# First block of a fused convolution and feed-forward kernel: one third of the taps moved from VectorE to TensorE

## The chip, the cores and the metric

One core of a Trainium2 chip. The metric is the device time of one execution in microseconds; a kernel's time is the median of its runs. The profile's span is the time from the first to the last instruction, in most runs 1.6 to 1.9 us less than the device time. The granted clock is the share of TensorE's full clock that the profile records (0.50 is half clock).

## The reference

A depthwise causal convolution with seven taps over the sequence (the taps are a softmax of a small weight, one set per head), then a feed-forward layer with SiLU. 32768 tokens, 192 channels, 2048 hidden units. x and weight are float32; w_in and w_out come as float64, and the kernel turns their 64-bit words into float32 itself ("rounding" below).

```python
w = softmax(weight)                          # 8 heads x 7 taps
x_pad = concat([zeros(B, 6, D), x], axis=1)  # causal, B=8, S=4096, D=192
out[b, s, c] = sum_k w[head(c), k] * x_pad[b, s + k, c]
h = out.reshape(B * S, D) @ w_in             # 192 x 2048
return (h * sigmoid(h)) @ w_out              # 2048 x 192
```

## The kernel before

The tokens are worked off in 32 blocks of 1024. A block's channels are split in three thirds (k = 0, 1, 2) of 64; two halves of the block's tokens lie in partitions 0 to 63 and 64 to 127. For blocks 1 to 31 everything runs beside the products of the block before. For block 0 nothing can: it has to be loaded, transposed, convolved and copied out while the weights are loaded and rounded. The change touches that head only. Its parts:

```python
def turn_in(b, k):      # VectorE: transpose third k of block b, nats -> xts
def conv(b, k, i):      # tap i; tap 0 on ScalarE (blocks 0, 1), the rest on VectorE
    src = xts[b][:, k, i : i + TB]
    dst = nats[b][:, k, :, :]                # in place of the loaded data
    ... scalar_tensor_tensor(out=dst, in0=src, scalar=tap, in1=dst, mult, add)
def spread(b, k):       # 4 DMAs of 128 KB: the convolved third to both row halves (dup)
    for n in range(2):
        for e in range(2):
            nc.sync.dma_start(out=dups[b][R*e : R*e+R, n, k, :], in_=src[R*n : R*n+R, :])
def load_in(j, queue):  # 4 DMAs of 192 KB: raw words of quarter j of w_in
def round_in(j, k):     # VectorE, a little ScalarE: raw words -> wr[j]; after the last piece
    ...                 # of a quarter, 2 GpSimd DMAs ws[j] <- wr[j] (halves swapped)
def up_plain(0, 0):     # block 0, quarter 0: third by third into 8 PSUM banks
    for k, (a, n) in order:                  # k outermost for quarter 0
        for e in range(2):
            nc.tensor.matmul(hs[a, n, e], rows(wr[j], e)[:, a, k, :], rows(d, e)[:, n, k, :], ...)
... # (cut)
for k in range(NK):
    if k == 0:
        turn_in(0, 0)
        conv(0, 0, 0)
    for i in range(1, K):
        conv(0, k, i)
    spread(0, k)
    if k < NK - 1:
        for j in ((1, 2), (3,))[k]:
            load_in(j, nc.sync)
        turn_in(0, k + 1)
        conv(0, k + 1, 0)
    round_in(0, k)
round_in(1)
for j in range(NJ):
    up_plain(0, j)
    ...
```

In the trace the nc.sync queue issues in this order: dup of the first third, weights of quarters 1 and 2, dup of the second third, weights of quarter 3, a small copy (tail, 4.5 KB), dup of the last third. In the text, "dup" is the set of four copies of one convolved third, a copy "lands" when its completion is reported, and each float32 product makes two records in the profile.

Of the kernel before, what the change touches and what calls it, by code (L numbers as in the profile page):

```python
# [9 lines left out]
F32 = mybir.dt.float32  # L10
I32 = mybir.dt.int32
AF = mybir.ActivationFunctionType
ALU = mybir.AluOpType
# [4 lines left out]
def kernel(  # L18
# [24 lines left out]
    nc = tc.nc  # L43
# [3 lines left out]
    H, K = weight.shape  # L47
    NT = B * S
    DFF = moe_w_in.shape[1]
    P = 128  # L50
    R = 64
    NK = D // R
    grp = D // H
    pad = K - 1
    TB = 512
# [16 lines left out]
    gpool = ctx.enter_context(tc.tile_pool(name="gp", bufs=2 * NJ))  # L72
    upool = ctx.enter_context(tc.tile_pool(name="up", bufs=13))
# [29 lines left out]
    def pin(ins):  # L103
        return tc.keep_in_program_order(ins)
# [8 lines left out]
    vec, act = Pinned(nc.vector), Pinned(nc.scalar)  # L113

    def bank():
        return psum.tile([P, TB], F32, tag="ps", name="ps")

    nats, xts, gs = {}, {}, {}

    def load(b, ks=range(NK)):  # L120
# [14 lines left out]
        out=wexp.rearrange("p h k -> p (h k)"),  # L135
        in_=weight.rearrange("(o h) k -> o (h k)", o=1).to_broadcast([P, H * K]),
# [5 lines left out]
    for k in range(NK):  # L142
        nc.gpsimd.dma_start(
            out=xts[0][R:P, k, 0:pad], in_=x0[:, k, :], allow_slow_non_contiguous=True
# [11 lines left out]
    wr = [const.tile([P, 2, NK, P], F32, name=f"wr{j}") for j in range(NJ)]  # L156
# [5 lines left out]
    def raw_tile(key):  # L162

        pool, tag = (gpool, "g") if key in (("i", 2), ("i", 3)) else (tpool, "t")
        raws[key] = pool.tile([P, 4 * TB], I32, tag=tag, name="raw")[:, 0 : 2 * WC]
        return raws[key]

    def load_in(j, queue):
        raw = raw_tile(("i", j)).rearrange("p (a k c) -> p a k c", a=2, k=NK)
        for e in range(2):  # L170
            for a in range(2):
                c = 2 * P * (NM * a + 2 * j + e)
                queue.dma_start(
                    out=raw[R * e : R * e + R, a, :, :], in_=in32[:, :, c : c + 2 * P]
                )
# [53 lines left out]
    def round_in(j, k=None):  # L229

        words = raws["i", j].rearrange("p (a k c t) -> p a k c t", a=2, k=NK, t=2)
        if k is None:
            rounded(
                wr[j].rearrange("p a k c -> p a (k c)"),
                words.rearrange("p a k c t -> p a (k c) t"),
                j < 2,
            )
        else:
            rounded(wr[j][:, :, k, :], words[:, :, k], j < 2)
        if k in (None, NK - 1):  # L240

            del raws["i", j]
            for e in range(2):
                nc.gpsimd.dma_start(
                    out=ws[j][R * e : R * e + R], in_=wr[j][R - R * e : 2 * R - R * e]
                )
# [41 lines left out]
    for e in range(2):  # L288
        half = hot[R * e : R * e + R]
        for sign, base in ((1, 0), (-1, grp - 1)):  # L290
            nc.gpsimd.affine_select(
                out=half,
                in_=half,
                compare_op=ALU.is_ge,
                fill=0.0,
                base=base,
                pattern=[[sign * R, NK], [-sign * grp, H]],
                channel_multiplier=sign,
            )
    wred = const.tile([P, H], F32, name="wred")  # L300
    taps = const.tile([P, NK, K], F32, name="taps")
    each = const.tile([P, NK, K, H], F32, name="each")
# [22 lines left out]
    def turn_in(b, k):  # L325
        if k == 0 and b:
            xt = xts[b] = xpool.tile([P, NK, pad + TB], F32, tag="xt", name="xt")
            if b * TT % S == 0:
                nc.gpsimd.memset(xt[0:R, :, 0:pad], 0.0)
            else:  # L330
                nc.gpsimd.tensor_copy(xt[0:R, :, 0:pad], tails.pop(b))
        xt = xts[b]
        pin(
            nc.vector.transpose(  # L334
                xt[:, k, pad : pad + TB], nats[b][:, k, :, :].rearrange("p k c -> p (k c)")
            )
        )
        if k == NK - 1:
            if b:
                nc.sync.dma_start(out=xt[R:P, :, 0:pad], in_=xt[0:R, :, TB : TB + pad])  # L340
            if (b + 1) * TT % S:
                tails[b + 1] = xpool.tile([R, NK, pad], F32, tag="tail", name="tail", bufs=2)
                nc.sync.dma_start(out=tails[b + 1], in_=xt[R:P, :, TB : TB + pad])

    def conv(b, k, i):

        src = xts[b][:, k, i : i + TB]
        dst = nats[b][:, k, :, :].rearrange("p k c -> p (k c)")
        tap = taps[:, k, i : i + 1]
        if i == 0 and b < 2:  # L350
            pin(nc.scalar.activation(dst, src, AF.Copy, scale=tap))  # L351
        elif i == 0:
            pin(nc.vector.tensor_scalar(dst, src, scalar1=tap, scalar2=None, op0=ALU.mult))
        else:
            pin(
                nc.vector.scalar_tensor_tensor(  # L356
                    out=dst, in0=src, scalar=tap, in1=dst, op0=ALU.mult, op1=ALU.add
                )
            )

    def spread(b, k):

        if k == 0:
            dups[b] = xpool.tile([P, 2, NK, TB], F32, tag="dup", name="dup")
        src = nats[b][:, k, :, :].rearrange("p k c -> p (k c)")
        for n in range(2):
            for e in range(2):
                nc.sync.dma_start(
                    out=dups[b][R * e : R * e + R, n, k, :], in_=src[R * n : R * n + R, :]
                )  # L370
# [17 lines left out]
    def rows(t, e):  # L388
        return t[R * e : R * e + R]

    def g_tile(b, j, a):
        if (b, j, a) not in gs:
            gs[b, j, a] = gpool.tile([P, 2, 2, TB], F32, tag="g", name="g")
        return gs[b, j, a]

    def up_plain(b, j):

        d = dups[b]
        outs = [(a, n) for a in range(2) for n in range(2)]
        hs = {(a, n, e): bank() for a, n in outs for e in range(2)}  # L400
        order = [(k, o) for k in range(NK) for o in outs]
        if j:
            order = [(k, o) for o in outs for k in range(NK)]
        for k, (a, n) in order:
            for e in range(2):
                nc.tensor.matmul(  # L406
                    hs[a, n, e],
                    rows(wr[j], e)[:, a, k, :],
                    rows(d, e)[:, n, k, :],
                    start=k == 0,  # L410
                    stop=k == NK - 1,
                )
            if k == NK - 1:
                for e in range(2):
                    g = g_tile(b, j, a)
                    act.activation(g[:, n, e, :], hs[a, n, e], AF.Silu)
# [308 lines left out]
            store(0, cols)  # L725


    for k in range(NK):
        if k == 0:
            turn_in(0, 0)  # L730
            conv(0, 0, 0)
        for i in range(1, K):
            conv(0, k, i)
        spread(0, k)
        if k < NK - 1:
            for j in ((1, 2), (3,))[k]:
                load_in(j, nc.sync)
            turn_in(0, k + 1)
            conv(0, k + 1, 0)
        round_in(0, k)  # L740
    round_in(1)
    for j in range(NJ):
        up_plain(0, j)
        if j + 2 < NJ:
            round_in(j + 2)
            load_out(j, nc.sync)
        else:
            round_out(j + 2 - NJ)
            load_out(j, nc.sync)
        if j == 1:  # L750
            load(1)
# [63 lines left out]
```

## Time and profile before

| | before |
|---|---|
| median, 3 runs | 2420.47 us (2420.43 to 2420.83) |
| TensorE busy | 99% of the span, without a pause from 37.73 us to the last blocks |
| head, 0 to 37.73 us | three batches of products, at 16.66, 27.34 and 33.47 us |

How to read it: nothing after 37.73 us can change through an edit to block 0's convolution, so the effect of the change is the shift of that one moment. A sharp mark for it in every profile is the start of the first down projection (68.83 us before): from there to the end of the span all kernels below take 2349.4 to 2350.2 us. The lines are in the prediction.

### The profile page before, as it was taken

To read this page: it belongs to the slowest core of one execution; us is meant where nothing else is said; L and a number is where in the kernel's file an instruction comes from. 1 tells how busy PE (TensorE), PEld (TensorE's weight loads), DVE (VectorE), ACT (ScalarE), POOL (GpSimd) and SP (SyncE) were. 2 spreads that over 40 slices of the span, in tenths; PEclk is the share of its full clock that TensorE was granted. 3 is DMA by queue.
4 is the path that set the end of the run, shared out by engine and by line. 5 is a ranking of instruction groups with operands and counts; after the bars stand their busy time and mean duration, and the time that the engine had idled before them with its cause. 6 is when DMAs were issued, how large, how long until landed. Compare 5 with 4: busy or idle time off the path is not lost.

```text
span 2418.9 us, 43131 instructions
## 1 busy us (share of the span) xinstructions
PE 2388.1 (99%) x17776; PEld 936.7 (39%) x17776; DVE 2073.5 (86%) x2821; ACT 990.7 (41%) x1857; POOL 69.8 (3%) x98
## 2 busy tenths in 40 slices
PE   6999999999999999999999999999999999999998
PEld 3334433334433344333443333443334433334433
DVE  8889888898888888888988889888889888898876
ACT  3234533345433345333454334543334533345432
POOL 3300000000000000000000000000000000000000
PEclk9999999999999999999999999999999999999999
DMA  8321222222222212222222222122222222222220
GB/s 157 75 45 38 39 44 53 44 43 38 36 53 51 42 32 43 46 53 40 40 40 40 53 47 45 33 36 53 53 41 40 36 45 53 43 41 40 36 40 14
DMA packets 454085, 111.65 MB, mean 46 GB/s; under 512 B 423936, under 2 KB 429056, under 8 KB 453888
## 3 DMA queue, kind: packets, MB, share of 16 engines
q1 hardware_dynamic: 450064, 106.89, 23.8%
q8 instruction: 139, 2.28, 0.4%
q0 software_dynamic: 480, 1.58, 0.3%
q10 hardware_dynamic: 3344, 0.42, 0.1%
q14 instruction: 58, 0.48, 0.1%
HBM read 31.49 MB, written 25.17 MB: 23 GB/s over the span
## 4 chain that ended last, share of the span: by engine, by line
PE 98%; DVE 1%; ACT 0%; DMA 0%; SPq 0%; issue 0%; POOLq 0%; POOL 0%; ACTq 0%; DVEq 0%
PE ps L442 49%; PE ps L513 46%; PE ps L541 2%; PE ps L406 1%; DVE nat L356 0%; DMA nat<-in_x_dram 0%; SPq L127 0%; DVE two L111 0%; ACT two L111 0%; ACT g L111 0%; DVE cmb L111 0%; DVE osb L111 0%; DVE xt L334 0%; ACT nat L351 0%; ACT L111 0%
## 5 line engine op out<-in xcount | busy, mean ns | idle before, releaser
L442 PE MATMUL ps<-dup,ws 64*128 64x512 f32 x2480 | 869.9, 589 | 0.0
L513 PE MATMUL ps<-g,wo 128*32 128x512 f32 x2984 | 662.2, 592 | 0.0
L466 DVE TENSOR_TENSOR g<-u,ps 128x512 f32<-128x512 f32 x744 | 485.5, 679 | 119.2 <-PE ps L442 89.9
L442 PE MATMUL ps<-win,wr 64*128 64x512 f32 x1488 | 567.7, 589 | 0.0
L513 PE MATMUL ps<-t,wo 128*32 128x512 f32 (+1 forms) x4464 | 500.7, 450 | 0.0
L463 ACT ACTIVATE g<-g 128x512 f32<-128x512 f32 x744 | 444.6, 631 | 97.2 <-DVE g L466 97.2
L442 PEld LDWEIGHTS ps<-dup,ws 64*128 64x128 f32 x2480 | 363.0, 187 | 292.0 <-issue 277.9
L513 PE MATMUL ps<-t,wx 128*32 128x512 f32 x2976 | 452.9, 592 | 0.0
L356 DVE SCALAR_TENSOR_TENSOR nat<-xt,taps,nat 128x512 f32<-128x512 f32 x576 | 432.0, 750 | 18.7 <-ACT nat L351 3.8
L442 PE MATMUL ps<-dup,wr 64*128 64x512 f32 x992 | 419.9, 596 | 0.0
L457 ACT COPY u<-ps 128x512 f32<-128x512 f32 x496 | 278.1, 589 | 228.7 <-PE ps L442 225.8
L580 ACT COPY cmb<-ps 96x512 f32<-96x512 f32 x30 | 17.5, 582 | 805.5 <-PE ps L513 805.5
L483 DVE TENSOR_TENSOR t<-g,t 128x1024 f32<-128x1024 f32 x248 | 303.4, 1223 | 18.7 <-PE ps L513 8.3
L483 DVE TENSOR_TENSOR t<-g 128x1024 f32<-128x1024 f32 x248 | 299.6, 1219 | 23.0 <-PE ps L513 23.0
L442 PEld LDWEIGHTS ps<-win,wr 64*128 64x128 f32 x1488 | 233.4, 187 | 175.5 <-issue 147.2
L513 PEld LDWEIGHTS ps<-t,wo 128*32 128x32 f32 x4464 | 178.3, 110 | 222.6 <-issue 204.6
L442 PE MATMUL ps<-win,ws 64*128 64x512 f32 x496 | 242.2, 589 | 0.0
L513 PE MATMUL ps<-g,wx 128*32 128x512 f32 (+1 forms) x1512 | 234.6, 585 | 0.0
L513 PEld LDWEIGHTS ps<-t,wx 128*32 128x32 f32 x2976 | 121.9, 110 | 277.6 <-issue 268.4
L592 DVE TENSOR_TENSOR cmb<-cmb,ps 96x512 f32<-96x512 f32 x150 | 102.3, 682 | 135.3 <-ACT u L577 133.2
L442 PEld LDWEIGHTS ps<-dup,wr 64*128 64x128 f32 x992 | 160.5, 187 | 128.2 <-issue 114.3
L513 PEld LDWEIGHTS ps<-g,wo 128*32 128x32 f32 x2984 | 169.4, 110 | 98.3 <-issue 98.3
(66 smaller groups left out, 1206.4 us busy)
## 6 DMA issues: line engine op xcount, KB each, us to landing
dup<-nat SPq DMA_DIRECT2D x384, 128.0 KB, 2.3
nat<-in_x_dram SPq DMA_DIRECT2D x382, 64.0 KB, 2.4
out_dram<-osb SPq DMA_DIRECT2D x376, 64.0 KB, 2.0
raw<-in_moe_w_in_dram SPq DMA_DIRECT2D x16, 192.0 KB, 5.7
raw<-in_moe_w_out_dram SPq DMA_DIRECT2D x8, 384.0 KB, 3.7
ws<-wr POOLq DMA_DIRECT2D x8, 192.0 KB, 3.3
xt<-xt SPq DMA_DIRECT2D x31, 4.5 KB, 1.9
tail<-xt SPq DMA_DIRECT2D x24, 4.5 KB, 1.9
```

The lines of the kernel that those rows point to most:

```text
L356: nc.vector.scalar_tensor_tensor(out=dst, in0=src, scalar=tap, in1=dst, op0=ALU.mult, op1=ALU.add)
L406: nc.tensor.matmul(hs[a, n, e], rows(wr[j], e)[:, a, k, :], rows(d, e)[:, n, k, :], start=k == 0, stop=k == NK - 1,)
L442: nc.tensor.matmul(bk[b, m, bn], rows(w, half), rows(v, half), start=first, stop=True, skip_group_check=True,)
L457: pin(copy(u, bk[b, m, "1"]))
L463: pin(nc.scalar.activation(g, g, AF.Silu))
L466: pin(nc.vector.tensor_tensor(g, us.pop((b, m, i)), bk[b, m, bn], op=ALU.add))
L483: pin(nc.vector.tensor_tensor(t[i // 2][:, i % 2, :], u, v, op=ALU.subtract))
L513: nc.tensor.matmul(accs[b][i][SQ * q : SQ * q + SQ, to], lhs[:, e, SQ * k : SQ * k + SQ], rhs[:, e, ts(q, TB // 4) if i == 5 else to], sta ...
L541: nc.tensor.matmul(acc[k][R * n : R * n + R, :], wo[j][:, a, e, R * k : R * k + R], gs[b, j, a][:, n, e, :], start=j == 0 and a == 0 and e ...
L580: pin(nc.scalar.copy(c[0], acc[0][0:n, :]))
L592: pin(nc.vector.tensor_tensor(out_, u, v, op=ALU.add))
```

## The change

Intent: VectorE is busy all through the head. Six of its taps (the second third) become seven products on TensorE with diagonal matrices (taps on the diagonal), summed in PSUM; ScalarE makes the diagonals and copies the sum back. TensorE stood idle there. The second third is transposed after four taps of the first, so that TensorE can start early.

```diff
+    one_hot = upool.tile([P, TB], F32, tag="u", name="one_hot")[:, 0:P]
+    nc.gpsimd.memset(one_hot, 1.0)
+    for sign in (1, -1):
+        nc.gpsimd.affine_select(out=one_hot, in_=one_hot, ...)   # cut: leaves the diagonal
 ... (the products of up_plain are held in program order: pin(...))
-    for k in range(NK):
-        if k == 0:
-            turn_in(0, 0)
-            conv(0, 0, 0)
-        for i in range(1, K):
-            conv(0, k, i)
-        spread(0, k)
-        if k < NK - 1:
-            for j in ((1, 2), (3,))[k]:
-                load_in(j, nc.sync)
-            turn_in(0, k + 1)
-            conv(0, k + 1, 0)
-        round_in(0, k)
+    turn_in(0, 0)
+    conv(0, 0, 0)
+    diag = gpool.tile([P, K, P], F32, tag="g", name="diag")
+    for i in range(K):
+        act.activation(diag[:, i, :], one_hot, AF.Copy, scale=taps[:, 1, i : i + 1])
+    for i in range(1, 5):
+        conv(0, 0, i)
+    turn_in(0, 1)
+    for i in range(5, K):
+        conv(0, 0, i)
+    spread(0, 0)
+    for j in (1, 2):
+        load_in(j, nc.sync)
+    by_pe = bank()
+    for i in range(K):
+        pin(nc.tensor.matmul(by_pe, diag[:, i, :], xts[0][:, 1, i : i + TB],
+                             start=i == 0, stop=i == K - 1))
+    round_in(0, 0)
+    turn_in(0, 2)
+    conv(0, 2, 0)
+    round_in(0, 1)
+    act.copy(nats[0][:, 1, :, :].rearrange("p k c -> p (k c)"), by_pe)
+    spread(0, 1)
+    load_in(3, nc.sync)
+    for i in range(1, K):
+        conv(0, 2, i)
+    spread(0, 2)
+    round_in(0, 2)
     round_in(1)
```

More of the change, by code (lines that the diff above doesn't have):

```diff
@@ L299 @@
             )
+    one_hot = upool.tile([P, TB], F32, tag="u", name="one_hot")[:, 0:P]
+    nc.gpsimd.memset(one_hot, 1.0)
+    for sign in (1, -1):
+        nc.gpsimd.affine_select(
+            out=one_hot,
+            in_=one_hot,
+            compare_op=ALU.is_ge,
+            fill=0.0,
+            base=0,
+            pattern=[[-sign, P]],
+            channel_multiplier=sign,
+        )
     wred = const.tile([P, H], F32, name="wred")
@@ L405, in up_plain @@
             for e in range(2):
-                nc.tensor.matmul(
-                    hs[a, n, e],
-                    rows(wr[j], e)[:, a, k, :],
-                    rows(d, e)[:, n, k, :],
-                    start=k == 0,
-                    stop=k == NK - 1,
+                pin(
+                    nc.tensor.matmul(
+                        hs[a, n, e],
+                        rows(wr[j], e)[:, a, k, :],
+                        rows(d, e)[:, n, k, :],
+                        start=k == 0,
+                        stop=k == NK - 1,
+                    )
                 )
@@ L725, in finish @@
             store(0, cols)
-    for k in range(NK):
-        if k == 0:
-            turn_in(0, 0)
-            conv(0, 0, 0)
-        for i in range(1, K):
-            conv(0, k, i)
-        spread(0, k)
-        if k < NK - 1:
-            for j in ((1, 2), (3,))[k]:
-                load_in(j, nc.sync)
-            turn_in(0, k + 1)
-            conv(0, k + 1, 0)
-        round_in(0, k)
+    turn_in(0, 0)
[13 more added lines that the diff above has]
+    for i in range(K):
+        pin(
+            nc.tensor.matmul(
+                by_pe, diag[:, i, :], xts[0][:, 1, i : i + TB], start=i == 0, stop=i == K - 1
+            )
+        )
+    round_in(0, 0)
[9 more added lines that the diff above has]
+    round_in(0, 2)
     round_in(1)
```

## The prediction

> **What bounds the kernel now.** I read the page first, for the bound and the chain that ended last. Columns: engine, busy us, share of the span, instructions; then shares of the span.
>
> ```profile
> span 2418.9 us, 43131 instructions
> PE 2388.1 (99%) x17776; PEld 936.7 (39%) x17776; DVE 2073.5 (86%) x2821; ACT 990.7 (41%) x1857; POOL 69.8 (3%) x98
> PE 98%; DVE 1%; ACT 0%; DMA 0%; SPq 0%; issue 0%; POOLq 0%; POOL 0%; ACTq 0%; DVEq 0%
> ```
>
> TensorE is the bound, so only its idle time can be won. Where is that? The busy time by stretch (us of the stretch, busy us of each engine with instructions, granted clock, DMA share, GB/s):
>
> ```profile
> 0.00:16.60 16.60, 0.00 (x0) 0.00 (x0) 10.35 (x28) 3.79 (x7) 3.41 (x13) 1.00 0.78 124
> 16.60:37.70 21.10, 15.80 (x48) 7.33 (x48) 20.14 (x39) 6.99 (x13) 3.50 (x5) 0.92 0.91 186
> 37.70:110.00 72.30, 72.27 (x336) 29.63 (x336) 66.84 (x82) 21.49 (x37) 37.11 (x50) 1.00 0.40 93
> 110.00:2400.00 2290.00, 2290.00 (x17262) 895.58 (x17264) 1967.74 (x2660) 953.89 (x1792) 24.32 (x29) 1.00 0.23 43
> ```
>
> From 37.7 us on TensorE does not stop until the last blocks. The change touches the first block alone, so its whole effect is how far the moment moves at which TensorE starts its unbroken run (37.73 us, when the products of the first quarter of the up projection are done). The timeline of the first 40 us, TensorE, VectorE (DVE) and the queues (start, length, what; idle before and what ended it):
>
> ```profile
> 16.66 5.90 PE L406 MATMUL ps<-dup,wr 64*128 64x512 f32 x16 [16.66 <-DVE wr L111]
> 27.34 5.83 PE L406 MATMUL ps<-dup,wr 64*128 64x512 f32 x16 [4.78 <-DMA dup<-nat]
> 33.47 4.07 PE L406 MATMUL ps<-dup,wr 64*128 64x512 f32 x16 [0.29 <-DMA dup<-nat]
> 37.73 31.17 PE L406 MATMUL ps<-dup,wr 64*128 64x512 f32 x144 [0.20 <-ACT g L111]
> ...
> 8.53 4.69 DVE L356 SCALAR_TENSOR_TENSOR nat<-xt,taps,nat 128x512 f32<-128x512 f32 x6 [0.84 <-ACT nat L351]
> 13.13 0.70 DVE L334 STREAM_TRANSPOSE xt<-nat 128x512 f32<-128x512 f32 x1
> 16.52 4.68 DVE L356 SCALAR_TENSOR_TENSOR nat<-xt,taps,nat 128x512 f32<-128x512 f32 x6
> 24.52 4.68 DVE L356 SCALAR_TENSOR_TENSOR nat<-xt,taps,nat 128x512 f32<-128x512 f32 x6
> ...
> 13.24 2.45 SPq L368 DMA_DIRECT2D dup<-nat  x4
> 15.74 5.26 SPq L173 DMA_DIRECT2D raw<-in_moe_w_in_dram  x8
> 21.23 2.43 SPq L368 DMA_DIRECT2D dup<-nat  x4
> 23.71 2.83 SPq L173 DMA_DIRECT2D raw<-in_moe_w_in_dram  x4
> 29.23 2.43 SPq L368 DMA_DIRECT2D dup<-nat  x4
> ...
> 32.06 1.28 POOL L244 DMA_DIRECT2D ws<-wr  x2 [27.31 <-DVE wr L111]
> ```
>
> Three batches of products (channel thirds k=0, 1, 2) each wait for their taps to be copied out (dup). VectorE works without a break, which invites the change. But the two later batches waited for a DMA, so I looked at the DMA in that stretch:
>
> ```profile
> DMA packets 2488, 2.74 MB, mean 211 GB/s; under 512 B 269, under 2 KB 2034, under 8 KB 2487
> DMA packets 1206, 1.47 MB, mean 211 GB/s; under 512 B 347, under 2 KB 886, under 8 KB 1206
> ```
>
> These are 15 to 28 us and 28 to 35 us: the same 211 GB/s in both, at 95 to 100% busy engines by the DMA view's slices. One by one, time from issue to landing is 2.3 us for the first dup copy (13.24, idle engines), 6.0 us for the first of the second third (21.23) and 4.1 us for the first of the last third (29.23, so landing at 33.33; the products follow at 33.47). The extra is queueing behind weight loads. So the head is bound by DMA volume from the first dup copy on, not by VectorE.
>
> **What the Trainium skill says.** "DMA: Bandwidth & Descriptors", section "Queues, rings and completion order": each DMA engine consumes the descriptors of one queue in ring order, and goes round-robin between queues packet by packet. The trace agrees: landings come in the order of issue (dup 27.2 to 28.8, weights 29.7 to 32.6, dup 33.3 to 34.4). "FP8 and Floating Point Precision", "TensorE Precision Notes": true FP32 takes 4 passes. The trace agrees: one fp32 product is two records, 144 records take 31.17 us, 0.216 each, and each uses half the array, so a product over the whole 128x128 array should take 2 x 0.43 = 0.86 us. "TensorE: Matmul & The Clock Gate", Part 1: the array starts at half clock and is released after about 3.4 us of activity. The trace agrees: the first batch's weight loads come 0.85 us apart until about 4.4 us in, then 0.45.
>
> **The change, part by part.**
>
> *VectorE loses* six taps of the second third: 6 x 0.785 (their spacing) = 4.7 us. The other taps stay. But the transpose of the second third moves ahead of taps 5 and 6 of the first third. Its input, the fourth load of the second third (issued 7.17, 5.1 us to landing), arrives at 12.29; four taps from 8.53 are through at 11.67. So VectorE stands 0.65 us and then transposes (0.63 to the next start): taps 5 and 6 start at 12.97 and 13.76 and the first third is ready at 14.5, not 13.2: **1.31 us later**.
>
> *TensorE gains* seven full-array products with diagonals, from about 13.1 us. Seven at 0.86 are 6.0 us warm; about half of that stretch is cold, so 8 to 9 us, end about 21.5. They are put ahead of the first batch, which ran at 16.66; it now runs about 21.5 to 24.9 instead of to 22.6. That hole existed anyway (4.78 us idle).
>
> *ScalarE gains* seven 128x128 activations (about 0.27 each by the 128x256 ones at 0.35, in an idle stretch) and a PSUM copy (0.59, the mean of other such copies), done at about 22.2. *GpSimd gains* a memset and two selects of 128x128, roughly 2 us after 3.5; two small selects for the taps come after one of them and end near 5.9 (4.75 before), and they are needed at 6.14. Up to 0.65 us more would vanish in the wait for the load.
>
> *The DMA queue* has the same transfers in nearly the same order (the small tail copy moves ahead of the second dup). It starts 1.31 us later: the first dup copies at 14.55, eight weight loads until 22.3, the tail, the second dup at about 22.9 (taps of this third are ready at 22.2, so TensorE's detour is just hidden), then weights, the last dup issued from about 28.5. Before, the last third's first dup landed 20.1 us after the first dup was issued (33.33 less 13.24), with never an empty queue. That sum is bytes over rate and stays: 14.55 + 20.1 = 34.65.
>
> *One transfer moves into this stretch.* The copies ws<-wr (2 x 192 KB, GpSimd's queue) are issued when the last piece of the first weights is rounded: at 32.06 before, mostly behind the last dup. VectorE is now ahead: first rounding 14.54 to 17.30, transpose to 17.93, second rounding to 20.70, taps of the last third to 25.30, rounding to 27.9. So ws<-wr goes out at about 28.1 and by round-robin shares the engines with the last weights and dup. 0.39 MB at about 0.26 MB per us is 1.5 us, some 0.2 of which was already ahead before: **+1.2 us**.
>
> So the last dup arrives from about 35.9 and, as before, TensorE needs 0.14 + 4.07 us from there: the unbroken run starts at about 40.1, against 37.73: +2.4 us. The middle batch (dup landing about 28.5, products cold, about 5.8 us, end 34.3) does not set it. ScalarE's wait of 0.20 goes away, because rounding, the table load and the first activations are no longer late. Sum: 2420.47 + 1.31 + 1.2, less 0.2 of that ScalarE wait = 2422.8; I put 2422.7. The engine orders of the two kernels are the same after the first block, except a few GpSimd and load issues.
>
> **The rivals.** (1) *VectorE was the bound of the head, and the saving arrives*: the last taps are ready at 25.3 instead of 29.2, so up to 3.9 us are won, about 2416.6 to 2417.5. For it: the chain of waits runs through the taps of VectorE there, and VectorE is busy 20.14 of 21.10 us. Against it: the last dup waited 4.1 us instead of 2.3 in a full queue. (2) *ws<-wr does not get in the way* (it is issued late, or its packets slip between): only the 1.31 us delay remains, about 2421.5. (3) *TensorE's products hold things up*: if all seven run cold they end at 25.1, the second dup is issued at about 25.7, the queue nearly runs dry, and 1 us more is lost: about 2424. (4) *The tap delay is smaller* because the load lands earlier: at best 0.6 us, the transpose alone: about 2422.0.
>
> **Range and chances.** Rivals 2 to 4 lie between 2421.5 and 2424; rival 1 I give about one in eight, and the runs before spread by 0.4 us. The range is 2420.0 to 2424.7. A change of 2% would be 48 us; the whole head is 38 us, so the time stays within 2% with 0.99.
>
> **What would show each step right or wrong.** First dup issue at about 14.5 (wrong if 13.3). Diagonal products from about 13.1, ending 20.8 to 22.5. Last taps ready at about 25.3, yet the last third's products start only near 36, with a wait for a DMA. ws<-wr issued near 28. DMA busy without a gap from 16 to 37 us. The prediction is wrong if the last third's products start before 33.5, above all if the last dup lands within about 2.5 us of issue: then the volume was not the bound and rival 1 holds.

## The result, and the profile after

Changed kernel: 2424.53 us, median of 6 runs (2422.84 to 2425.48); before 2420.51 (2420.43 to 2420.95, 6 runs). Ratio 1.0015, 95% interval 1.0002 to 1.0028. A ratio is the mean time of one kernel's runs over that of the other's in the same rounds, so not quite the ratio of the medians. By the rule of 2% the time is the same; by the interval the change costs 0.15%. The spread grew from 0.5 to 2.6 us.

The page of the changed kernel (the profiled run is one of its faster ones, 2423.16 us):

```profile
span 2421.5 us, 43167 instructions
PE 2395.2 (99%) x17790; PEld 937.1 (39%) x17790; DVE 2065.1 (85%) x2815; ACT 991.8 (41%) x1864; POOL 66.1 (3%) x101
```

The timeline of the changed kernel by engine, in the order of the lines before: TensorE (L759 are the diagonal products, L419 the up projection), VectorE (L346 transposes, L368 taps), the queue (L380 dup, L173 weights) and GpSimd's ws<-wr.

```profile
13.07 8.88 PE L759 MATMUL ps<-xt,diag 128*128 128x512 f32 x14 [13.07 <-DVE xt L346]
21.87 3.70 PE L419 MATMUL ps<-dup,wr 64*128 64x512 f32 x16
27.82 5.82 PE L419 MATMUL ps<-dup,wr 64*128 64x512 f32 x16 [2.25 <-DMA dup<-nat]
35.50 1.09 PE L419 MATMUL ps<-dup,wr 64*128 64x512 f32 x2 [1.85 <-DMA dup<-nat]
36.81 8.52 PE L419 MATMUL ps<-dup,wr 64*128 64x512 f32 x37 [0.22 <-DMA dup<-nat]
...
12.25 0.71 DVE L346 STREAM_TRANSPOSE xt<-nat 128x512 f32<-128x512 f32 x1 [0.67 <-DMA nat<-in_x_dram]
20.27 4.68 DVE L368 SCALAR_TENSOR_TENSOR nat<-xt,taps,nat 128x512 f32<-128x512 f32 x6
...
14.41 2.46 SPq L380 DMA_DIRECT2D dup<-nat  x4
22.98 2.48 SPq L380 DMA_DIRECT2D dup<-nat  x4
28.44 3.29 SPq L380 DMA_DIRECT2D dup<-nat  x4
...
27.98 1.37 POOL L244 DMA_DIRECT2D ws<-wr  x2 [0.32 <-issue]
```

What to see: VectorE is through with the last third's taps at 24.95 instead of 29.2 us, the intended gain. Yet the last third's products start at 35.50, two us later than before. The last dup was issued at 28.44 and its first part landed 6.9 us later (DMA view narrowed to that issue; 4.1 us before). The chain that ended last, in order of time, now runs through that wait; before it went through VectorE's taps:

```profile
22.98 4.70 DMA dup<-nat
27.69 1.03 DVE two L111 x2
29.04 7.73 DMA dup<-nat
36.81 34.70 PE ps L419 x158
```

The first down projection starts at 71.44 us, against 68.83: 2.61 us later, which is the whole difference of the two spans (2421.5 less 2418.9).

### The profile page after: what moved, and what is told of

Its sections match the earlier page's. It is cut to its first block, busy times and chain, and to the rows that moved or that the text cites. A ratio compares the mean times of both kernels' runs of the same rounds, so it can differ in the third digit from the quotient of the medians.

```text
span 2421.5 us, 43167 instructions
## 1 busy us (share of the span) xinstructions
PE 2395.2 (99%) x17790; PEld 937.1 (39%) x17790; DVE 2065.1 (85%) x2815; ACT 991.8 (41%) x1864; POOL 66.1 (3%) x101
## 4 chain that ended last, share of the span: by engine, by line
PE 98%; DMA 1%; DVE 1%; issue 0%; ACT 0%; SPq 0%; POOLq 0%; POOL 0%; ACTq 0%; DVEq 0%
PE ps L456 49%; PE ps L527 46%; PE ps L555 2%; PE ps L419 1%; DMA dup<-nat 1%; DMA nat<-in_x_dram 0%; DVE two L111 0%; DVE nat L368 0%; DVE cmb L111 0%; DVE osb L111 0%; DVE xt L346 0%; DVE mh L111 0%; ACT two L111 0%; SPq L127 0%; POOLq L843 0%
## 5 line engine op out<-in xcount | busy, mean ns | idle before, releaser
L368 DVE SCALAR_TENSOR_TENSOR nat<-xt,taps,nat 128x512 f32<-128x512 f32 x570 | 427.5, 750 | 18.5 <-ACT nat L363 3.8
L497 DVE TENSOR_TENSOR t<-g 128x1024 f32<-128x1024 f32 x248 | 299.8, 1220 | 22.8 <-PE ps L527 22.8
```

The lines of the kernel that those rows point to most:

```text
L368: nc.vector.scalar_tensor_tensor(out=dst, in0=src, scalar=tap, in1=dst, op0=ALU.mult, op1=ALU.add)
L497: pin(nc.vector.tensor_tensor(t[i // 2][:, i % 2, :], u, v, op=ALU.subtract))
```

## The experiments

Theory: the head is bound by the volume on the DMA queue ahead of the last dup copies. The change delays the queue's start (wait of the transpose) and moves ws<-wr into it. Rivals: VectorE is the bound; ws<-wr does no harm; the diagonal products hold things up. The runs brought a fourth: TensorE's clock.

| run | what | median us (range) | before in the same job |
|---|---|---|---|
| after | the change | 2424.53 (2422.84 to 2425.48) | 2420.51 |
| e1 | transpose after all six taps | 2423.71 (2423.18 to 2424.28) | 2420.82 |
| e2 | ws<-wr behind the last dup | 2421.02 (2420.82 to 2421.19) | 2420.82 |
| e3 | e1 and e2 | 2420.21 (2419.24 to 2421.51) | 2420.82 |
| e4 | e2, late weight loads | 2416.37 (2416.19 to 2416.63) | 2420.82 |
| e5 | the change again | 2424.58 (2423.17 to 2426.21) | 2420.56 |
| e6 | before, with the late loads of e4 | 2420.64 (2420.30 to 2421.36) | 2420.56 |
| e7 | e1 with filler products | 2422.18 (2421.39 to 2424.04) | 2420.56 |
| e8 | e4 with the order of e1 | 2416.30 (2415.85 to 2416.87) | 2420.56 |
| e9 | three diagonal products (wrong result) | 2423.10 (2423.03 to 2423.24) | 2420.54 |
| e10 | e8 with 4 zero products first | 2416.54 (2415.84 to 2416.88) | 2420.54 |
| e11 | e8 with 11 zero products first | 2415.89 (2415.43 to 2416.14) | 2420.55 |

All results were correct but that of e9.

**e1: the order of the taps.**

```diff
-    for i in range(1, 5):
-        conv(0, 0, i)
-    turn_in(0, 1)
-    for i in range(5, K):
+    for i in range(1, K):
         conv(0, 0, i)
+    turn_in(0, 1)
```

> The transpose of the second third goes back behind all six taps of the first third; all else as in the changed kernel. DMA theory: the first dup copies are issued at about 13.2 us instead of 14.4, the whole queue moves with them, and the last third's products start about 1.2 us earlier than in the changed kernel (35.5 to 34.3), although the diagonal products on TensorE start about 0.8 us later; span about 2420.3, against 2421.5. Rival 3 (TensorE's late products hold things up): the products end later, so it is no better or up to 0.8 us slower than the changed kernel.

Half of it came. The first dup was issued at 13.25 us and the last third's products started at 34.24, as the DMA theory said. But the span was 2422.6, not 2420.3. The timeline of e1, then the busy time by stretch of e1 (the number after the engines is the granted clock):

```profile
26.67 4.37 PE L419 MATMUL ps<-dup,wr 64*128 64x512 f32 x16 [1.35 <-DMA dup<-nat]
34.24 26.33 PE L419 MATMUL ps<-dup,wr 64*128 64x512 f32 x104 [3.20 <-DMA dup<-nat]
```

```profile
34.00:41.00 7.00, 6.76 (x15) 4.87 (x17) 6.93 (x10) 2.87 (x5) 5.68 (x6) 0.51 0.55 149
```

A granted clock of 0.51: after TensorE's pause of 3.2 us, nearly the whole stretch from 34 to 41 us ran at half clock. The array was slowed just where it was at last on the path. The prediction had no half clock there.

**e2: ws<-wr out of the way.**

```diff
-                nc.gpsimd.dma_start(out=ws[j][...], in_=wr[j][...])
+                (nc.gpsimd if j else nc.sync).dma_start(out=ws[j][...], in_=wr[j][...])
```

> The changed kernel, but the first ws<-wr copies are issued on the same queue as dup, behind the last dup copies, so that they cannot share the engines with them. DMA theory: the last four dup copies land at about 34.3 to 35.8 us instead of 35.4 to 37.7, and the unbroken run of TensorE starts about 1.5 us earlier; span about 2420.0. Rival 2 (ws<-wr slips between the packets): less than 0.4 us of change.

The dup copies landed at 34.4, 34.95, 35.5 and 36.0 us instead of 35.4, 36.8, 37.3 and 37.7, and the down projection started at 69.72, 1.72 us sooner (span 2419.1); expected were 1.5. Rival 2 is out. The median fell by 3.5 us, more than the landings explain: this kernel's runs also lie within 0.4 us of each other. In its trace, after the diagonal products, the clock is at half from 28.4 to 31.8 us alone, on the middle batch.

```profile
34.54 25.81 PE L419 MATMUL ps<-dup,wr 64*128 64x512 f32 x117 [0.85 <-DMA dup<-nat]
```

The pause ahead of the last third is 0.85 us here, and no second one follows at 36.8.

**e3: both edits.**

> Both edits, the order of the taps and ws<-wr behind the last dup. DMA theory: the two costs add, about 2.7 us off the changed kernel, so the span comes out at about 2418.8, within 0.5 us of the kernel before: VectorE's 4.7 us are still not won, because the volume in front of the last dup is as before. Rival 1 (VectorE bounds the head): 2415 to 2416.

Median 2420.21; the costs do add up, and VectorE's saving still does not arrive. The profiled run was 1.3 us better than expected (span 2417.5) and has full clock from 18.4 us on. The four runs fall in two pairs: 2419.24 and 2419.31 with a mean granted clock of 0.999, 2421.11 and 2421.51 with 0.998.

**e4: nothing in front of the last dup.** On top of e2, the loads of quarters 2 and 3 move behind the last dup (and the queue's order is held):

```diff
     spread(0, 0)
-    for j in (1, 2):
-        load_in(j, nc.sync)
+    load_in(1, nc.sync)
 ...
     spread(0, 1)
-    load_in(3, nc.sync)
 ...
     spread(0, 2)
+    for j in (2, 3):
+        load_in(j, nc.sync)
     round_in(0, 2)
```

> The changed kernel with ws<-wr behind the last dup and the loads of the third and fourth quarter of the weights (1.6 MB) also behind the last dup; order on the queue held. DMA theory: nothing queues in front of the last dup any more, it lands about 2.3 to 2.6 us after issue (issued about 25.1, landed 27.4 to 30), the products of the three thirds follow each other with little idle time, and the unbroken run starts when the second quarter's weights are rounded, about 33.6 us: span about 2414.8 and time about 2416.3, faster than both kernels by about 4 us, with less spread. If VectorE or TensorE were what holds the changed kernel back: no better than 2419.

2416.37 against an expected 2416.3; ratio 0.9982 (0.9967 to 0.9997). The DMA view narrowed to the last dup's first issue gives 2.2 us to landing. The timeline of e4, TensorE and queue:

```profile
21.58 11.20 PE L419 MATMUL ps<-dup,wr 64*128 64x512 f32 x48
33.89 26.45 PE L419 MATMUL ps<-dup,wr 64*128 64x512 f32 x122 [1.12 <-DVE wr L111]
...
22.30 5.33 SPq L380 DMA_DIRECT2D dup<-nat  x8
27.67 5.29 SPq L173 DMA_DIRECT2D raw<-in_moe_w_in_dram  x8
```

All three thirds run back to back, 48 records in 11.2 us. The wait is now for rounded weights, that is for VectorE. The volume ahead of the last dup was the bound, and VectorE the next one, 4 us behind. What e4 takes away has two parts: in the change the last third's taps were ready at 24.95 us, the dup copies had to let the weights be issued first until 28.44 us, and then took 6.9 us to land; in e4 the last dup is issued at 25.25 us and lands in 2.2. The two are not separated here.

**e5: the change again.** No edit.

> The changed kernel once more, unedited, for its spread and a second profile. Its six runs lay between 2422.8 and 2425.5 us while the kernel before kept within 0.5. Clock theory: TensorE's pauses in the head (2.25 and 1.85 us in the profile) let the clock fall back to half for a stretch of 3.4 us whose place is a matter of chance; where it falls on the last third's products a run is about 2425, where it falls on the middle third's it is about 2423. A profile of a long run should show half clock in the 34 to 41 us range. Rival: the DMA is what varies, and the last dup's landing moves by 2 us between the two profiles.

Median 2424.58. Its profile is of a 2424.58 us run, 1.4 us longer than the first profile's. The first part of the last dup landed at 35.16 us and the last at 37.60, against 35.36 and 37.73 in the first profile: the DMA did not vary. The clock did. By stretch, first the profile of the change shown above, then that of e5:

```profile
34.00:41.00 7.00, 5.28 (x21) 2.46 (x23) 6.93 (x10) 3.62 (x8) 4.37 (x5) 1.00 0.72 184
```

```profile
34.00:41.00 7.00, 5.53 (x13) 2.40 (x15) 6.93 (x10) 2.91 (x5) 4.63 (x5) 0.77 0.68 175
```

Both have half clock for 3.4 us on the middle third, where it costs nothing; e5 has a second such stretch from 37.8 to 41.2 us. The time from the last third's first product to the first down projection puts the cost in one number for each profile: 35.9 us for the change (with a short wait for dup in it, 0.22 us), 37.7 in e5, 38.4 in e1; 35.2 in e2, where no clock was lost there. Over the eleven runs of the change the mean granted clock and the time go together only loosely (0.999: 2422.8, 2423.2, 2424.6; 0.997: 2424.6 to 2426.2), since that mean also contains a half-clock stretch of 5 to 8 us at the very end. So it is shown for the profiled runs; for the others it is the likely cause. After the clock's first release, the half-clock stretches in the heads of all profiles last 3.4 us (before, change, e2, both of e5) or 6.8 us (e1, e6, e9, e10).

**e6: the late loads without the diagonal products.** The kernel before, with ws<-wr and the weight loads as in e4.

> The kernel before (taps of all thirds on VectorE) with the same late weight loads and late ws<-wr as e4. If the gain of e4 needs both the shorter queue and the diagonal products: no gain here, because the second quarter's weights are rounded on VectorE at 37.6 us whatever the DMA does; 2420.4, within 0.4 us of the kernel before. If the shorter queue alone made e4 fast: about 2416.5 to 2417.5.

2420.64: no gain. The timeline of e6, TensorE and VectorE:

```profile
31.72 37.55 PE L406 MATMUL ps<-dup,wr 64*128 64x512 f32 x160 [3.44 <-DVE wr L111]
...
36.38 0.96 DVE L111 SCALAR_TENSOR_TENSOR wr<-mh,two 128x768 f32<-128x768 f32 x1
```

The last third's products start 1.75 us earlier than before, but the second quarter's weights are ready only at 37.3 us (37.6 before), and its products cannot start without them. So at most 0.4 us could be won on the 37.73 us of the kernel before. The profile does not show TensorE waiting for these weights, though. After its pause of 3.44 us the clock was at half from 30.6 to 37.4 us, so the last third's products held TensorE until 38.1 us (by stretch, the granted clock is the third number from the end):

```profile
31.70:37.40 5.70, 5.68 (x14) 4.18 (x16) 5.57 (x8) 4.72 (x7) 0.00 (x0) 0.50 0.96 208
```

At full clock they would have been done at about 35.7 us (an estimate from the 4.0 us that they take in e4), and VectorE would have been the limit. So the kernel before had two limits side by side, DMA and VectorE, both near 37.6 us. The change removed one; e6 removes the other; only both together (e4) pay.

**e7: filler against the clock.** e1, plus products with an all-zero tile added into an open sum:

```diff
+            if j == 0 and (a, n) == outs[-1] and k < NK - 1:
+                for _ in range((1, 3)[k]):
+                    for e in range(2):
+                        pin(nc.tensor.matmul(hs[0, 0, e], rows(wr[0], e)[:, 0, 0, :],
+                                             rows(zeros, e), start=False, stop=False))
```

> e1 with filler for TensorE: after the first third's products one pair, and after the second third's three pairs of products with an all-zero tile are added into a sum that is open anyway (nothing changes in the result), to keep the array busy in the pauses of 1.35 and 3.2 us. Clock theory: no half clock after 20 us, the last third's products take about 4 us instead of 7, and e1's 2423.7 falls to about 2421.0, although TensorE has more work. Rival (the landing alone sets it): 2423.5 or later.

Half a miss: 2422.18, 1.5 us better than e1 with more work for TensorE, but not 2421.0. In the profile the clock stays full, and the stretch from the last third to the down projection is 35.1 us instead of 38.4. But the diagonal products ended at 22.8 us there instead of 21.7 (their cold part varies), so the second dup was issued at 23.47 instead of 22.33 and the last dup landed 1.0 us later. One of the four runs was still at 2424.04.

**e8: e4 with the order of e1.**

> e4 with the transpose of the second third behind all six taps, as in e1. e4 is now held by VectorE (the rounded second quarter at 33.9 us), and VectorE stands about 0.65 us before the early transpose. If that wait goes without harm elsewhere: about 0.5 us faster than e4, 2415.9. If the later start of the diagonal products counts instead (they end up to 0.5 us later): 2416.4 to 2416.9.

2416.30, no clear difference from e4. VectorE is ready earlier (32.8 us), but TensorE starts the diagonal products 0.6 us later than in e4 and now has no pause at all from 13.9 us on; their 9.1 us are on the path.

**e9: three products instead of seven** (taps 0, 3 and 6 only).

```diff
-    for i in range(K):
+    for i in (0, 3, 6):
         pin(nc.tensor.matmul(by_pe, diag[:, i, :], ...))
```

> Wrong on purpose: the changed kernel with three of the seven diagonal products, so four taps of the second third of the first block are missing and the result differs there. DMA theory: TensorE is through with them about 3.5 us sooner (18 us instead of 21.9), but the second dup still waits for its turn in the queue and the last dup lands at 35 to 38 us as in the changed kernel: median within 2422.5 to 2425.5, no gain. Rival 3 (the products hold the second and last third up): about 1 to 3 us faster than the changed kernel, 2421.5 or less.

2423.10. TensorE was ready 3.3 us sooner and only waited longer:

```profile
28.06 6.25 PE L419 MATMUL ps<-dup,wr 64*128 64x512 f32 x16 [5.52 <-DMA dup<-nat]
35.36 1.09 PE L419 MATMUL ps<-dup,wr 64*128 64x512 f32 x2 [1.05 <-DMA dup<-nat]
```

The last third starts at 35.36 (35.50 in the change), and the span is 2421.4 (2421.5 in the first profile). Rival 3 is out for the changed kernel. That the median is 1.4 us lower than the change's fits the clock: in the one profile the half-clock stretch, 26.0 to 32.8 us, ends before the last third. For the other three runs this is not shown.

**e10 and e11: warm before the diagonal products.** e8, plus all-zero products into the same bank, later overwritten: four in e10, eleven in e11.

```diff
     by_pe = bank()
+    for _ in range(4):       # e11: 11
+        pin(nc.tensor.matmul(by_pe, zeros[:, 0:P], zeros, start=True, stop=True))
```

> e8 with four products of all-zero tiles on TensorE before the diagonal ones (their sum is overwritten), from about 2 us on, so that the array may be at full clock when the diagonal products start at 13.9. In e8 TensorE did not pause from 13.9 us on, so the cold products (9.1 us, 6.0 at full clock) are on its path. Clock theory: if the clock is still full at 13.9, the products take about 6 us, TensorE then waits for VectorE's rounded second quarter (32.8 us) and the time is 0.3 to 0.8 us below e8, about 2415.7. If the array has fallen back by then[...]: equal to e8 within 0.3 us.

> e10 with eleven all-zero products in place of four. In e10 the four ended at 7.3 us, the array stood 7.0 us, and the clock was back at half when the diagonal products began at 14.3. Each further zero product at full clock takes 0.86 us, so eleven end at about 13.3. Clock theory: full clock through the diagonal products, which then take about 6 us instead of 8.8, and TensorE is through with them at about 20; the unbroken run is then set by VectorE's rounded second quarter at about 32.8 to 33.2 us: 0.2 to 0.5 us faster than e8, about 2415.9. If full clock does not help the products: as e8 or slower.

e10: no gain, 2416.54. The four ended at 7.3 us, TensorE stood 7.0 us, and the diagonal products took 8.8 us, cold again. e11 is sized by that, and its products are at full clock as the theory said:

```profile
1.44 11.33 PE L757 MATMUL ps<-zeros 128*128 128x512 f32 x22 [1.44 <-POOL zeros L142]
14.03 6.25 PE L760 MATMUL ps<-xt,diag 128*128 128x512 f32 x14 [1.26 <-issue]
20.21 11.60 PE L421 MATMUL ps<-dup,wr 64*128 64x512 f32 x48
33.10 31.17 PE L421 MATMUL ps<-dup,wr 64*128 64x512 f32 x144 [1.29 <-DVE wr L111]
```

The diagonal products take 6.25 us, and the wait is again for VectorE. 2415.89 us, ratio to the kernel before 0.9981 (0.9964 to 0.9997): the lowest median here, 4.7 us below the kernel before and 8.6 below the change. A gain over e8 is not shown: the ranges overlap (e8 from 2415.85 us), and the two ran in different jobs.

## Why the prediction was right

It said 2422.7 (2420.0 to 2424.7); measured 2424.53, in the range, 0.2 us below its upper end. The chain of waits was right: no gain, the queue ahead of the last dup as the reason, a loss of some us. The size was not: it forecast 2.2 us of loss, and the medians differ by 4.0. That the median still fell in the range is in part luck: the upper end came from another rival (all diagonal products cold, 2424), and three of the eleven runs of the change lie above it (2425.12, 2425.48, 2426.21). Step by step, against the profile of the change, one of its faster runs:

- *The whole effect is the shift of one moment.* Right: +2.61 us at the down projection, +2.6 us of span; +2.4 predicted. The second quarter's products began at 40.03 us (40.1 predicted), by two errors that cancel: the first dup part landed 0.5 us earlier than predicted, and from the last third's first product to there took 4.5 us instead of 4.07, with waits for the later dup parts.
- *The first dup 1.31 us later.* It was 1.17 (14.41 less 13.24); VectorE's wait for the load was 0.67 us (0.65 predicted). e1 took it away, and the first dup went back to 13.25.
- *Diagonal products end at about 21.5.* They ended near 21.9; half clock until 18.4 us. e9 shows that they are hidden.
- *Volume ahead of the last dup sets its landing.* Right, and shown by e4: 2.2 us to landing instead of 6.9 once the queue is empty. First landing 35.36 (35.9 predicted), after an issue at 28.44 (28.5). That the queue was never empty is not exact: in the DMA view of 15 to 28 us before, two slices from about 17.0 to 17.6 us are only 10 and 40% busy, against the 95 to 100% that the prediction read.
- *ws<-wr goes out near 28.1 and costs 1.2 us.* Issued at 27.98. e2 gained 1.7 us at the down projection, so the term was too small. The first dup part lost 0.96 us by ws<-wr (35.36 against 34.40 in e2), the last 1.7 (37.73 against 36.01): the copies also spread the four, with a further short wait. The prediction's rate of 0.26 MB per us matches a stretch of 0.6 us alone (256 GB/s from 32.1 to 32.7 us, a view that it does not show); at the 211 GB/s that it had read, 0.39 MB take 1.9 us, 1.7 without the 0.2 (an estimate).
- *Rival 1, VectorE was the bound.* Wrong as a forecast for this change, but its mechanism is real, and "by DMA volume [...], not by VectorE" was half right: before, the second quarter's weights were rounded at 37.6 us, just when the last third's products ended (37.5), and e6 shows that with the DMA out of the way they are still not ready before 37.3 us. The chain of waits before led through VectorE and ScalarE because it came last by 0.2 us; the DMA limit a moment earlier could not be seen in it.
- *Missing: the clock.* The prediction counted half clock for the diagonal products and the middle batch, where it is hidden, and full clock for the last third (4.07 us). After the longer pauses ahead of the middle and last third the clock fell back, and where in the head it does is not fixed; e5 and e1 have it on the last third, worth 1.8 and about 3 us there (half of 3.4 and of 6.8 us would be 1.7 and 3.4). This is the likely reason for the median 1.8 us above the prediction and for the spread.
- *Without effect.* GpSimd's memset and two selects took 0.8 us, not roughly 2.

## What to carry to other kernels

Two limits can end within a fraction of a microsecond of each other, and a chain of waits shows only the later one. Before work is moved off a busy engine, ask of the next wait what it would be with that engine infinitely fast: here a copy that already took 4.1 us to land instead of 2.3 told of the queue in front of it, and reordering the queue and moving the taps paid only together. A pause added ahead of TensorE costs twice when the clock falls back after it (in e1, 3.2 us of pause, then 6.8 us at half clock).

## What the Trainium skill lacked or had wrong

- "TensorE: Matmul & The Clock Gate", Part 1, puts the fall to half clock after at least one idle window of about 3.4 us. Here shorter pauses were enough: 2.25 us in the change (half clock from 28.6 us) and 2.08 us in e5 (from 37.8 us, 2.5 us after the products had resumed). The length alone does not decide: in e6 a pause of 2.42 us, ended at 24.55 us, left the clock full.
- The same page has no word on whether products of zeros release the clock. They do: in e11 it was full from 4.7 us on, 3.3 us after the first all-zero product, and stayed so until the last blocks.
- "FP8 and Floating Point Precision", TensorE Precision Notes, gives four passes for FP32 but no measured time of such a product. Over the whole array with 512 columns: 6.25 us for seven products, 0.89 each, at full clock.
- "DMA: Bandwidth & Descriptors", Bandwidth, measures 341 GB/s for a transfer of 1 MB. No page has the rate of a full queue of such mixed 128 and 192 KB copies in pieces of 1 to 2 KB: 211 GB/s here.
